# A fused attention, max-out and PReLU kernel: another order of the last batch's gate units and splits, and the first scores in two pairs of PSUM banks

## The chip, the cores and the metric

The kernel runs on one core of one Trainium2 chip. The metric is the device time of one execution in microseconds, from start to end, all loads and stores included. Smaller is better. In the texts below TensorE (PE in the rows) multiplies, VectorE (DVE), ScalarE (ACT) and GpSimd (POOL) work elementwise, and SP issues the DMAs.

## What is computed

Three layers follow one another. First comes attention over 4 batches, 8 heads, 576 positions and head width 64. Half of the heads look at the last 32 positions, the other half at every 32nd position:

```python
rel = pos[:, None] - pos[None, :]
mask_local = (rel >= 0) & (rel < stride)
mask_strided = (rel >= 0) & (pos[None, :] % stride == pos[:, None] % stride)
scores = np.where(masks, scale * q @ k.T, -1e9)
attn = softmax(scores) @ v
```

Its result, 2304 tokens by 512, goes through a max-out layer and then through a PReLU layer:

```python
h = np.maximum(np.maximum(x @ w1, x @ w2), x @ w3)    # 512 -> 768
y = h @ w_out                                         # 768 -> 512
g = np.maximum(y @ w_in, 0) + alpha * np.minimum(y @ w_in, 0)   # 512 -> 2048
out = g @ w_out2                                      # 2048 -> 512
```

All of it is float32. The kernel splits each factor of a large product into a high half (a cast, mostly on ScalarE) and a low half (a subtraction, mostly on VectorE), and takes three products, high by high, high by low and low by high.

## The kernel before

**The first stage, planned.** The attention of all batches, the first layer of batches 0 to 2 and the preparing of the weights are written as tasks. Each task has an engine, a cost, a due position, things it needs and gives, and ring slots (such as the 8 PSUM banks) it takes. The class `Weave` lists them in an order by simulating the engines with these costs (L108), and each engine then executes its tasks in that order. Costs count in nanoseconds: `COST = (250, 600, 500, 500)` are those of the local scores, local values, strided scores and strided values on TensorE; after a task of TensorE the plan waits 300, after one of ScalarE or VectorE 350, after a load 2300.

**A unit of strided attention** (`strided_tasks`, L439) is a batch and a pair of heads. Its scores are 24 matmuls (48 in the records, since a float32 matmul appears twice) into two PSUM banks, one for each head. They come in three groups i of two column blocks t each. For each group there is a mask task on VectorE (L475: add the mask, keep the row's maximum; four instructions) and an exponential task on ScalarE (L487: four instructions). Then follow normalisation, transposes, the product with the values, and the split of the result into x tiles, one for each half (`hf`) of the batch's positions and each 128 of the 512 model columns (`cc`). Before the first units' scores TensorE is given matmuls on a constant tile whose result nobody reads (L228). The first unit is u = (0, 2), batch 0 and `cc` 2; the second is (0, 3).

**Raw weights** arrive as 64-bit words and are taken apart on ScalarE and VectorE (L590 to L607) and then split (L283, L286). Three raw tiles are in flight.

**The last batch** (`last_net`, L844) follows the plan and is written out by hand, because its first layer is done in two ways. The gates of the first two of six f blocks are direct: a unit (hf, f, g) is one of 12 groups of 12 matmuls (L740), with `GATES_LAST` giving the order of (hf, f) and g running over the three gate matrices. Unit g = 0 is copied on ScalarE (L749), units 1 and 2 are maxima on VectorE that read the PSUM bank (L751), and after unit 2 the result h is split (L233, L236). The other four f blocks use Strassen's scheme with seven products of half size instead of eight (L922, 6 matmuls each), in the order 11, T2, 21, T3, T4, T1, 22. For them VectorE makes sums of x tiles, 16 operations called row sums (L863), four after each of the units 1 to 4. Then `make(m)` (L881) splits the eight sums: m = 0, 1 are T1 for the two halves of the model columns, 2, 3 are T2, 4, 5 are T3 and 6, 7 are T4. T4 is written into the x tiles of half 1 that the direct gate units read (`xt[b, i, 1]`). After unit n the calls are `make(n - 4)` for n from 4 to 9, and `make(6)`, `make(7)` follow the last unit. SP loads the Strassen weights after units 3, 5 and 7 (L896), and further ones later (`load_factors`).

**Beside it**, from the loop at L1126, which counts the same units n, the second layer's input of block 1 is made ready: loads into the tiles `xs` are issued at n = 2 and have to wait until the row sums and T1's split have read these tiles; at n = 8 GpSimd is given four subtractions (L1000), and from n = 10 on, every other n, a split whose low half is GpSimd's too (L236, `xst`).

**After the Strassen products** come 8 output products (L762, 18 matmuls each, a PSUM bank each), beside which ScalarE and VectorE split the second layer's first block (x2, L1150). The second layer (L1378 and on) fills the rest of the time.

**PSUM** is a ring of 8 banks (`bank()`, L274) up to the second layer; an allocation waits for the readers of the one eight before it.

## Time and profile before

| | us |
|---|---|
| median of 3 runs | 730.28 |
| lowest, highest | 729.89, 732.47 |
| the profiled execution, whole | 729.32 |
| its span, first to last instruction | 727.5 |
| TensorE busy | 716.7 |
| VectorE busy | 617.9 |
| ScalarE busy | 446.7 |
| mean granted TensorE clock, share of full | 0.997 |

The span is that of one execution. A busy TensorE is not TensorE at its pace: matmuls overlap, and their ends are modelled, so a stretch is read by how many matmuls it holds. In a row of a timeline, what stands in brackets at the end is how long the engine was idle before, and which instruction ended that. A line such as L236 can be that of a helper which several places call; the names of the tiles tell them apart.

### The profile page before, as it was taken

Reading aid. Unit: us, or ns where it says so; the run is one execution under the profiler, and the core shown is the slowest. Engines: PE = TensorE matmul, PEld = TensorE weight load, DVE = VectorE, ACT = ScalarE, POOL = GpSimd, SP = SyncE. Lnnn points to the kernel's source line nnn. Section 1 sums busy time; section 2 is a strip of 40 time slices with the busy share of each in tenths; the row PEclk is TensorE's granted clock in tenths of the full one; section 3 lists DMA queues with packets and bytes.
Section 4 is the critical chain, followed back from the end, with each engine's and each line's share of the span. In section 5 each row is a group of like instructions: output and inputs, shape, how many; then the busy total and the mean of one; then the engine's idle time right before and its main releaser. Section 6 shows DMA issues by size and latency. Waiting matters only on the chain.

```text
span 727.5 us, 18169 instructions
## 1 busy us (share of the span) xinstructions
PE 716.7 (99%) x6682; PEld 698.2 (96%) x6682; DVE 617.9 (85%) x1680; ACT 446.7 (61%) x1180; POOL 29.5 (4%) x53
## 2 busy tenths in 40 slices
PE   8999999999999999989999999999999999999998
PEld 5899999999999999989999999999999999999997
DVE  6988987987978997779878988979988888888896
ACT  7988976876776684233356575535566644656561
POOL 2000000000000000066000000000000000000000
PEclk9999999999999999999999999999999999999999
DMA  8787499878999778798998799999789999868362
GB/s 297 266 278 229 167 325 336 308 274 298 327 346 348 251 267 299 244 347 314 362 347 320 258 332 330 403 391 371 243 296 318 377 390 365 295 231 268 106 190 77
DMA packets 90089, 214.46 MB, mean 295 GB/s; under 512 B 11152, under 2 KB 41360, under 8 KB 90000
## 3 DMA queue, kind: packets, MB, share of 16 engines
q1 hardware_dynamic: 90000, 213.30, 83.2%
q8 instruction: 53, 0.87, 0.5%
q14 instruction: 36, 0.29, 0.1%
HBM read 157.16 MB, written 56.10 MB: 293 GB/s over the span
## 4 chain that ended last, share of the span: by engine, by line
PE 93%; DVE 2%; ACT 2%; DMA 2%; issue 0%; SPq 0%; ACTq 0%; DVEq 0%
PE ph L1378 24%; PE bank L740 23%; PE po L1179 15%; PE bank L762 11%; PE bank L922 4%; PE po L1185 4%; PE ph L1179 4%; PE po L1189 2%; PE bank L426 1%; PE bank L352 1%; PE bank L465 1%; ACT es L487 1%; PE bank L535 1%; DMA raw<-in_w 1%; DMA w<-ws 1%; DMA wo<-w 1%
## 5 line engine op out<-in xcount | busy, mean ns | idle before, releaser
L1378 PE MATMUL ph<-x,w 128*128 128x384 f32 x990 | 199.4, 336 | 0.0
L740 PE MATMUL bank<-x,w 128*128 128x288 f32 x1440 | 197.5, 296 | 0.6 <-ACT w L283 0.4
L740 PEld LDWEIGHTS bank<-x,w 128*128 128x128 f32 x1440 | 191.8, 188 | 2.2 <-ACT w L283 0.6
L1378 PEld LDWEIGHTS ph<-x,w 128*128 128x128 f32 x990 | 166.6, 188 | 0.8
L1179 PE MATMUL po<-w,g 128*128 128x256 f32 x936 | 135.8, 282 | 0.0
L1179 PEld LDWEIGHTS po<-w,g 128*128 128x128 f32 x936 | 130.1, 190 | 0.3
L1384 DVE TENSOR_TENSOR c<-ph,c 128x384 f32<-128x384 f32 x165 | 89.3, 553 | 31.1 <-PE ph L1378 30.4
L1172 ACT CAST g<-c 128x384 fp32r<-128x384 f32 x93 | 47.0, 505 | 91.3 <-DVE c L1362 52.3
L762 PE MATMUL bank<-h,w 128*128 128x288 f32 x576 | 80.1, 297 | 0.0
L762 PEld LDWEIGHTS bank<-h,w 128*128 128x128 f32 x576 | 77.0, 188 | 0.4
L286 DVE TENSOR_TENSOR w<-word,w 128x512 fp32r<-128x512 f32 x100 | 63.5, 643 | 14.0 <-ACT w L283 13.4
L283 ACT CAST w<-word 128x512 fp32r<-128x512 f32 x100 | 57.7, 588 | 25.7 <-DMA wp<-w 7.5
L1322 ACT ACTIVATE c<-c 128x384 f32<-128x384 f32 x96 | 50.5, 526 | 33.2 <-DVE c L1384 32.0
L1323 ACT ACTIVATE c<-c,nalpha 128x384 f32<-128x384 f32 x96 | 59.3, 617 | 3.1
L1327 DVE SCALAR_TENSOR_TENSOR c<-c 128x384 f32<-128x384 f32 x96 | 53.0, 552 | 5.9 <-ACT c L1323 5.9
L1173 DVE TENSOR_TENSOR g<-c,g 128x384 fp32r<-128x384 f32 x96 | 52.8, 550 | 0.9 <-ACT g L1172 0.5
L1173 DVE TENSOR_TENSOR g<-k,g 128x384 fp32r<-128x384 f32 x72 | 37.0, 551 | 7.4 <-ACT g L1172 7.4
L1185 PE MATMUL po<-w,g 128*128 128x512 f32 x120 | 42.8, 395 | 0.0
L830 DVE TENSOR_TENSOR t<-bank,t 128x288 f32<-128x288 f32 x72 | 32.6, 452 | 9.0 <-PE bank L740 5.6
L590 ACT ACTIVATE word<-raw 128x512 f32<-128x512 f32 x56 | 37.2, 678 | 4.1 <-DMA raw<-in_w 3.1
L922 PE MATMUL bank<-x,w 128*128 128x288 f32 x252 | 36.3, 305 | 2.6 <-DVE x L236 1.4
L922 PEld LDWEIGHTS bank<-x,w 128*128 128x128 f32 x252 | 35.3, 196 | 3.5 <-DVE x L236 2.1
(123 smaller groups left out, 905.3 us busy)
## 6 DMA issues: line engine op xcount, KB each, us to landing
w<-wh SPq DMA_DIRECT2D x72, 512.0 KB, 5.2
raw<-in_w SPq DMA_DIRECT2D x50, 512.0 KB, 5.2
w<-wo SPq DMA_DIRECT2D x48, 512.0 KB, 5.9
w<-wp SPq DMA_DIRECT2D x36, 512.0 KB, 6.3
wh<-w SPq DMA_DIRECT2D x24, 512.0 KB, 4.9
xd<-xst SPq DMA_DIRECT2D x28, 384.0 KB, 3.5
x<-xd SPq DMA_DIRECT2D x28, 384.0 KB, 8.4
ws<-w SPq DMA_DIRECT2D x12, 512.0 KB, 5.1
```

The source lines that it names most:

```text
L283: (nc.scalar.copy if e == "ACT" else nc.vector.tensor_copy)(out_, in_)
L286: nc.vector.tensor_tensor(out=out_, in0=x, in1=y, op=ALU.subtract)
L740: nc.tensor.matmul(acc, words["gate", f, g][:, wi, cc * P:(cc + 1) * P], xt[b, cc, hf][:, xi, :], start=n == 0, stop=n == 3 * NCC - 1)
L762: nc.tensor.matmul(acc, words["mix", f][:, wi, dc * P:(dc + 1) * P], st["h", hf, f][:, xi, :], start=n == 0, stop=n == 3 * NF1 - 1)
L922: nc.tensor.matmul(bank_, w[:, wi, off + c * P:off + (c + 1) * P], factors[name, c][:, xi, :], start=m == 0, stop=m == 5)
L1173: return g, lambda: nc.vector.tensor_tensor(out=g[:, 1], in0=x, in1=g[:, 0].bitcast(F32), op=ALU.subtract)
L1179: nc.tensor.matmul(bank[:, NH * half:NH * (half + 1)], g[:, gi, t * P:(t + 1) * P], w[:, wi, off:off + NH], start=first and i == 0, stop=l ...
L1185: nc.tensor.matmul(bank.rearrange("p (s n) -> p s n", n=NH), g[:, 0, t * P:(t + 1) * P], w[:, :, off:off + NH], start=first, stop=last)
L1323: nc.scalar.activation(a, a, AF.Copy, scale=nalpha[:, f:f + 1])
L1327: nc.vector.scalar_tensor_tensor(out=a, in0=h, scalar=0.0, in1=a, op0=ALU.max, op1=ALU.add)
L1378: nc.tensor.matmul(bank, words["h", n, i][:, wi, off + c * P:off + (c + 1) * P], x2h[blk, k, c][:, xi, :], start=m == 0, stop=m == 5)
L1384: nc.vector.tensor_tensor(out=out_, in0=bank, in1=other, op=ALU.add)
```

## The change

It has two parts.

The first is in the last batch. `GATES_LAST` goes from (0,0), (1,0), (0,1), (1,1) to (0,0), (1,0), (1,1), (0,1), so that both blocks of half 1 are done after unit 8 of 0 to 11. The splits of the token sums come after units 4 (one), 5 (two), 6 (two), 7 (one), 9 (one) and 10 (one) instead of one after each of the units 4 to 9 and two after the last.

The second is in the strided units. For the first one, (0, 2), the scores become two tasks, each with its own pair of PSUM banks: group 0 in the first, groups 1 and 2 in the second; a group's masks read the pair in which its scores are. For every strided unit the matmuls are now issued group by group instead of by g from 0 to 11.

```diff
--- before.py
+++ after.py
@@ -43,6 +43,7 @@
 WARM = 8
 UNREAD = {(0, 3): 2, (0, 0, 0): 2, (0, 1, 0): 3, ((0, 2), "t", 0): 4, ((0, 2), "s"): 2, ((0, 3), "s"): 3, (0, 0, 0, 0): 6}
 AFTER = {(1, 2): [("begun", 0, ("t", 0, 0, 0))]}
+PARTED = {(0, 2)}
 REDUCED = {(0, 2), (0, 3), (0, 0, 0), (0, 1, 0)}
 
 
@@ -446,34 +447,39 @@
         u = (b, cc)
         slack = 1500 if b else 0
         ek, qk, vk = ("es", u), ("q", b, cc), ("v", b, cc)
-        banks = [("sc", u, j) for j in range(2)]
-        cols = 6 * RW
-
-        def scores(_):
+        shares = ((0,), (1, 2)) if u in PARTED else ((0, 1, 2),)
+        banks = [[("sc", u, j, n) for j in range(2)] for n in range(len(shares))]
+
+        def scores(n):
             q, k = tl[qk]
-            sc = tl["sc", u] = [bank() for _ in range(2)]
-            unread(sc[0], UNREAD.get(u, 0))
-            tl[ek] = e_strided[turn[0] % 2]
-            turn[0] += 1
-            for name in ("mx", "ss", "sr"):
-                tl[name, u] = sm2.tile([P, 2, 6], F32, tag=name, name=name)
-            for g in range(12):
-                at = RW * min(g, NG2 - 1)
-                t = 2 * (g % 6 // 2) + g // 6
-                for j in range(2):
-                    rows = slice(D * j, D * (j + 1))
-                    nc.tensor.matmul(sc[j][D * (g % 2):D * (g % 2 + 1), RW * t:RW * (t + 1)],
-                                     q[rows, at:at + D], k[rows, at:at + RW], start=True, stop=True)
-
-        add((("PE", COST[2]),), scores, pos, needs=[qk], gives=[("sc", u)],
-            makes=[("bank", key) for key in banks] + [("es", ek)], uses=[qk], mode="scores")
+            sc = [bank() for _ in range(2)]
+            if n == 0:
+                unread(sc[0], UNREAD.get(u, 0))
+                tl[ek] = e_strided[turn[0] % 2]
+                turn[0] += 1
+                for name in ("mx", "ss", "sr"):
+                    tl[name, u] = sm2.tile([P, 2, 6], F32, tag=name, name=name)
+            for i in shares[n]:
+                tl["sc", u, i] = sc
+                for g in (2 * i, 2 * i + 1, 2 * i + 6, 2 * i + 7):
+                    at = RW * min(g, NG2 - 1)
+                    t = 2 * i + g // 6
+                    for j in range(2):
+                        rows = slice(D * j, D * (j + 1))
+                        nc.tensor.matmul(sc[j][D * (g % 2):D * (g % 2 + 1), RW * t:RW * (t + 1)],
+                                         q[rows, at:at + D], k[rows, at:at + RW], start=True, stop=True)
+
+        for n, part in enumerate(shares):
+            add((("PE", COST[2] * len(part) // 3),), lambda _, n=n: scores(n), pos,
+                needs=[qk] + ([("sc", u, 0)] if n else []), gives=[("sc", u, i) for i in part],
+                makes=[("bank", key) for key in banks[n]] + ([] if n else [("es", ek)]), uses=[qk], mode="scores")
         heads = (0, 1)
         for i in range(3):
             def masked(_, i=i):
                 for t in (2 * i, 2 * i + 1):
                     for j in heads:
                         nc.vector.tensor_tensor_reduce(
-                            out=tl[ek][:, j, t, :RW], in0=tl["sc", u][j][:, RW * t:RW * (t + 1)], in1=mask_s,
+                            out=tl[ek][:, j, t, :RW], in0=tl["sc", u, i][j][:, RW * t:RW * (t + 1)], in1=mask_s,
                             scale=-SCALE, scalar=3.0e38, op0=ALU.add, op1=ALU.min,
                             accum_out=tl["mx", u][:, j, t:t + 1])
                 if (u, i) == ((0, 2), 0):
@@ -486,7 +492,8 @@
                         sums = {} if u in REDUCED else dict(accum_out=tl["ss", u][:, j, t:t + 1])
                         nc.scalar.activation(e, e, AF.Exp, bias=tl["mx", u][:, j, t:t + 1], scale=-1.0, **sums)
 
-            add((("DVE", 4 * 133),), masked, pos, needs=[("sc", u)], gives=[("nm", u, i)], uses=banks + [ek])
+            add((("DVE", 4 * 133),), masked, pos, needs=[("sc", u, i)], gives=[("nm", u, i)],
+                uses=banks[i > 0 if u in PARTED else 0] + [ek])
             add((("ACT", 4 * (160 if u in REDUCED else 325)),), exponential, pos, needs=[("nm", u, i)],
                 gives=[("exp", u)], uses=[ek])
 
@@ -780,7 +787,7 @@
     GATES = [(0, 0), (0, 1), (0, 2), (1, 0), (0, 3), (0, 4), (1, 1), (0, 5), (1, 2),
              None, (1, 3), (1, 4), (1, 5), None]
     GATES_THEN = [what for what in GATES if what] + [None, None]
-    GATES_LAST = [(hf, f) for f in range(2 * NP // 3) for hf in range(2)]
+    GATES_LAST = [(0, 0), (1, 0), (1, 1), (0, 1)]
 
     def units(gates):
         hf = 0
@@ -890,14 +897,11 @@
                 for step in row_sums[:4]:
                     step()
                 del row_sums[:4]
-            if 4 <= n < 10:
-                make(n - 4)
+            for m in {4: (0,), 5: (1, 2), 6: (3, 4), 7: (5,), 9: (6,), 10: (7,)}.get(n, ()):
+                make(m)
             if n in (3, 5, 7):
                 load_factors(NP + n // 2)
             yield
-        for m in range(6, 8):
-            make(m)
-
         def add(out_, bank, other, op=ALU.add):
             nc.vector.tensor_tensor(out=out_, in0=bank, in1=other, op=op)
 
```

## Rows read from the trace of the kernel before

**Rows 1.** The page: busy time of each engine, share of the span, instructions.

```profile
PE 716.7 (99%) x6682; PEld 698.2 (96%) x6682; DVE 617.9 (85%) x1680; ACT 446.7 (61%) x1180; POOL 29.5 (4%) x53
```

**Rows 2.** Busy time by stretch: start:end length, engines (instructions), granted clock, DMA, GB/s.

```profile
0.00:35.00 35.00, 30.09 (x598) 23.87 (x602) 26.51 (x145) 28.68 (x99) 5.18 (x28) 1.00 0.81 279
35.00:291.60 256.60, 256.60 (x3157) 251.47 (x3149) 223.21 (x750) 190.35 (x607) 0.00 (x0) 1.00 0.84 290
...
310.65:317.50 6.85, 4.28 (x27) 3.35 (x25) 5.75 (x10) 3.39 (x10) 5.28 (x5) 0.99 0.96 364
317.50:321.00 3.50, 3.49 (x15) 3.49 (x16) 2.42 (x7) 1.05 (x3) 2.94 (x3) 0.52 0.99 396
```

**Rows 3.** Timeline, TensorE, the last batch's gate units: start, us, what, [idle before].

```profile
291.61 19.20 PE L740 MATMUL bank<-x,w 128*128 128x288 f32 x144
```

**Rows 4.** Timeline, TensorE, the first Strassen products.

```profile
310.65 2.68 PE L922 MATMUL bank<-x,w 128*128 128x288 f32 x19
313.83 0.67 PE L922 MATMUL bank<-x,w 128*128 128x288 f32 x3 [0.51 <-DVE x L236]
315.01 0.54 PE L922 MATMUL bank<-x,w 128*128 128x288 f32 x2 [0.51 <-DVE x L236]
316.73 0.40 PE L922 MATMUL bank<-x,w 128*128 128x288 f32 x1 [1.19 <-ACT x L233]
317.51 4.78 PE L922 MATMUL bank<-x,w 128*128 128x288 f32 x23 [0.37 <-DVE x L236]
```

**Rows 5.** Timeline, VectorE, the same stretch and just before.

```profile
307.72 0.45 DVE L751 TENSOR_TENSOR t<-bank,t 128x288 f32<-128x288 f32 x1
308.67 0.46 DVE L236 TENSOR_TENSOR h<-t,h 128x288 fp32r<-128x288 f32 x1 [0.50 <-ACT h L233]
...
312.52 2.44 DVE L236 TENSOR_TENSOR x<-t,x 128x288 fp32r<-128x288 f32 x2
314.88 1.01 DVE L751 TENSOR_TENSOR t<-bank,t 128x288 f32<-128x288 f32 x2
...
317.01 0.81 DVE L236 TENSOR_TENSOR x<-t,x 128x288 fp32r<-128x288 f32 x2
```

**Rows 6.** Timeline, GpSimd: first and third of its four subtractions.

```profile
311.26 1.02 POOL L1000 TENSOR_TENSOR t<-xs 128x384 f32<-128x384 f32 x1 [304.31 <-DVE t L751]
...
313.54 1.10 POOL L1000 TENSOR_TENSOR t<-xs 128x384 f32<-128x384 f32 x1
```

**Rows 7.** Timeline, ScalarE: T4's two high halves.

```profile
316.25 0.76 ACT L233 CAST x<-t 128x288 fp32r<-128x288 f32 x2
```

**Rows 8.** Timeline, VectorE and TensorE, the second layer's start.

```profile
364.30 0.55 DVE L236 TENSOR_TENSOR x<-xst,x 128x384 fp32r<-128x384 f32 x1
...
368.54 2.26 PE L1378 MATMUL ph<-x,w 128*128 128x384 f32 x12
```

**Rows 9.** Timeline, all engines, the first unit's scores and masks.

```profile
4.76 1.54 PE L465 MATMUL bank<-k,q 64*64 64x54 f32 x48
...
6.48 0.21 DVE L475 CUSTOM_DVE_ANT_0 es<-bank,mask_s 128x54 f32<-128x54 f32 x1 [5.48 <-PE bank L465]
...
7.14 0.92 PE L465 MATMUL bank<-k,q 64*64 64x54 f32 x48
...
8.11 0.21 DVE L475 CUSTOM_DVE_ANT_0 es<-bank,mask_s 128x54 f32<-128x54 f32 x1
...
17.12 0.95 DVE L286 TENSOR_TENSOR x<-bank,x 128x162 fp32r<-128x162 f32 x4 [0.55 <-ACT x L283]
```

**Rows 10.** Chain of work that ended last, first 35 us: start, us, what.

```profile
6.73 5.64 ACT es L487 x24
...
24.59 5.43 DMA raw<-in_w
...
32.02 1.62 PE bank L740 x10
```

## The prediction

> **What bounds the kernel now.** I read the page first: TensorE is busy for 99% of the span, VectorE for 85% [rows 1]. A kernel that is at its matmul pace nearly everywhere gains only where TensorE is not at that pace, so the second view is the busy time by stage [rows 2]. There the reader sees two places. In the first 35 us TensorE is busy 30.1 us, but with single small units and filler; until the first long run of gate products starts, the pace is set by the chain scores, masks, exponentials, weights. And in 310.65 to 317.50, where the last batch's Strassen products begin, it is busy 4.28 of 6.85 us, after which the granted clock is 0.52 for the next 3.5 us, that is near the lower level of 1.2 GHz against 2.4 GHz. From 35 to 291.6 us it is busy without a hole. The change touches exactly the two places, so I priced them and then asked whether a start won there reaches the end.
>
> **The matmul pace.** 144 gate products take 19.20 us, 0.1333 each [rows 3]. In 310.65 to 317.50 TensorE did 19 + 3 + 2 + 1 = 25 products [rows 4], worth 3.33 us: 3.5 us are lost to waiting. The slow clock costs (1 - 0.52) x 3.5 = 1.7 us more [rows 2]. Together 5.2 us is all that the second place can give back.
>
> **Why it waits there.** The waits are for the token sums' splits (VectorE L236): 0.51 and 0.51 us for the two of T3, then 1.19 for ScalarE's and 0.37 for VectorE's half of T4 [rows 4]. VectorE works in program order. Behind unit 5's maximum at 307.72 it splits T1, T2, takes two maxima, and gets to T3 only at 312.52; both T3 splits take 2.44 us instead of 2 x 0.46. Then come two maxima until 315.89, the low half of h, and at 317.01 T4 [rows 5]. The 2.44 us are GpSimd's doing: four subtractions run without a break from 311.26 on, some 1.15 us apart [rows 6], and VectorE's two-SBUF-input operations last until some 0.3 us after the running GpSimd one (312.52 + 2.44 = 314.96 against 313.54 + 1.10 = 314.64), while maxima that read PSUM keep their 0.45 to 0.5 pace.
>
> The Trainium skill (SBUF — State Buffer, section SBUF: two separate sides) calls this port pair an exclusive lock, held for the whole instruction, also against VectorE operations with two SBUF inputs. By that rule a caught split takes one GpSimd operation, 1.10 us; the row says 1.22, half of 2.44. The sum below goes by the row; by the rule, three caught splits would end 0.4 us sooner.
>
> **Part 1, the gate order and the splits.** Nothing is added or removed: 12 gate units, 16 row sums, 8 splits as before; no DMA is moved, and SP's loads at units 3, 5 and 7 keep their places. T1's first split stays at unit 4, which matters: the load of GpSimd's rows into the xs tiles waits for it, so GpSimd's start at 311.26 stays too (take that; were it bound to unit 8's maximum instead, it would start up to 0.8 us later, which helps). Up to 307.72 VectorE's order is unchanged. From there:
> - unit 5's maximum ends at 308.17; h's low half starts at 308.67 after the usual 0.50 wait for ScalarE [rows 5]. Then T1, T2, T2, T3 follow without maxima between. ScalarE gives a high half every 0.38 us at most (two in 0.76) [rows 7], VectorE takes 0.4 from start to start (two in 0.81) [rows 5]; T3's first low half starts at 310.4, unit 7's maximum at 310.75, T3's second at 311.1, done by 311.5, about when GpSimd starts.
> - TensorE needs T3 after three products, 18 x 0.1333 = 2.4 us behind 310.65: at 313.05. T3's two waits are gone, with 1.5 us of cover.
> - What is late next is T4, the fifth product, wanted at 313.85. Before it stand unit 8's maximum (to 311.95) and the low half of h (ready at 312.4), then T4's first split, unit 10's maximum and T4's second split. Three of these five have two SBUF inputs and fall into GpSimd's run. If the low half of h catches the end of GpSimd's first operation, the three end at about 312.9, 314.05 and 315.2; if it just misses it, one operation later, at 313.8, 314.95 and 316.1. With 0.3 us for the matmuls behind, T4 ends at 315.5 or 316.4 where the pace alone would give 314.65. The lost time is 0.9 to 1.8 us; I take the middle, 1.35: the rows don't say which it is, since low half and subtraction would start within 0.1 us of each other.
> - T4 may now be written early, since it overwrites x tiles of half 1 and those units end at unit 8. Behind T4's splits the maxima of units 10 and 11 come later than their own products by up to 6 us; who waits for them are the products that take their PSUM banks, eight allocations on: the last of this group at 316.8 and the first of the next at 317.6, against maxima done by 315.4 and 316.5. The cover is 1.1 us; without it the next group's first product would wait for unit 11's maximum.
> - The clock. Before, it fell after four idle stretches of 2.6 us in all within 313.3 to 317.5; now I expect two, of together 0.7 to 1.5 us. The first 35 us hold 4.9 us of idle time in pieces and keep 1.00 all through [rows 2]. So I take it that the clock holds, and keep its 1.7 us as a rival. The Trainium skill (TensorE: Matmul & The Clock Gate, section Why this matters for your kernels) warns only of a single long idle gap, by which the clock would hold here for sure; the trace disagrees, for its longest gap was 1.19 us and the clock fell all the same, so this rule is not used.
>
> Part 1 gives 5.2 - 1.35 = 3.9 us, between 3.4 and 4.3.
>
> **Does it reach the end?** Behind the Strassen products come the output products, then the second layer at 368.54. Its first product needs the x2 splits, the last of which that it reads runs at 364.30 to 364.85 [rows 8]. This leaves 3.7 us if those splits don't move at all; their loads are issued from TensorE's own progress, so they move with it for the most part. I take 0.2 off, with 0 to 0.7 as bounds: 3.7 us for part 1. After that TensorE has no hole of its own, and nothing takes the start back.
>
> **Part 2, the first unit's scores.** The 48 recorded matmuls take 1.54 us from 4.76, and the first mask starts at 6.48, after all of them [rows 9]. With a bank pair for the first third, the first four masks need 16 of 48, some 0.5 to 0.7 us: they start at 5.45 to 5.65 and the exponentials, 24 in a row from 6.73 [rows 10], about 0.85 us earlier. Masks 5 to 12 of the unit wait for the second pair at 6.48 as before, and ScalarE has four exponentials (0.94 us) to bridge. What is hidden: the second unit's masks start at 8.11 because its scores run at 7.14 to 8.06 [rows 9], and those wait for their loads; so VectorE gains nothing there. From 8.11 on VectorE's order has one hole, 0.55 us at 17.12, and that is a wait for ScalarE [rows 9]. ScalarE being 0.6 to 0.85 us early, this hole closes: 0.55 us. The chain from there goes over VectorE's word joins to the raw weights' load issued at 24.59, its landing 5.43 us later and the first dense products at 32.02 [rows 10], each of which starts when the one before ends. I take 0.5 us; 0 if the load lands when it did (the queue has other loads in it), 0.85 at most.
>
> The two added bank allocations move the ring by two. By the planner's own costs the two shares (166 + 333 for 500) bring the first masks and exponentials forward by 334 of its nanoseconds, but VectorE's tasks behind the second unit's scores keep their planned starts, and ScalarE's lead is used up at the next masks it must wait for: the order on each engine stays, worked out by hand. The ring's shift also moves the second layer's first two banks onto output units that are copied out earlier (the second and third of eight rather than the fourth and fifth), which helps if anything. The other units' changed order of groups costs nothing: a mask waits for the whole unit in any case.
>
> **Sum.** 3.7 + 0.5 = 4.2 us. The profiled execution's own time is 729.32 us (span 727.5 and 1.8 around it): 725.1. It stands 0.96 us below the median of the runs shown, 730.28, which is what a run is compared with: 726.1 us.
>
> **Rivals.**
> - *The clock falls again* in T4's shorter stall: 1.7 us less, 4.2 - 1.8 = 2.4 gained, 727.9. For it: two idle stretches remain, close together. Against: less than 60% of the idle time before. 0.15.
> - *The lock keeps the stall*: T3's second split is caught too, everything shifts by one more GpSimd operation, T4's second split ends at 317.1, as late as before, and the clock falls. Lost 2.75 + 1.7 instead of 5.2; with part 2, 1.3 us gained, 729.0. This is the skill's lock rule at its worst alignment; the row of 2.44 us shows it can hold two splits running. 0.12.
> - *Part 2 does nothing*, the load landing when it did: 726.6. 0.07.
> - *Slower*: my hand-worked plan is wrong, and the two shares put a load of values or of the next batch ahead of a raw weight load. One such load is 5.43 us from issue to landing [rows 10], and up to 6.1 with the queue full; it decides once the loss passes the 4.2 us gained: 730.3 - 3.7 + 6.1 = 732.7. Against it: nothing in the plan's first 9 us competes with those loads. 0.06.
>
> The forecast itself keeps 0.60, with 725.0 to 727.4 as its own range (3.4 + 0 - 0.7 up to 4.3 + 0.85).
>
> **How the numbers follow.** 0.5% is 3.65 us, about what a measurement of this kernel can tell from no change; it puts the line at 726.6, within the forecast's own range. Three quarters of the forecast lie below it, and half of the third rival: 0.60 x 0.75 + 0.07 x 0.5 = 0.48, rounded to 0.5. Slower by over 0.5% needs a loss of 7.3 us behind the gain: 0.03. The rest is within. The range for 8 in 10 goes from the forecast's best (4.3 + 0.85 and some scatter of the runs, 724.8) to the second rival (729.0).
>
> **What would show it.** In the profile after: the first mask at about 5.5 and the 24 exponentials from about 5.8; VectorE's 0.55 us hole gone and the first dense products near 31.5; no wait of TensorE for T3; its waits for T4 together below 1.6 us; granted clock 1.00 throughout 310 to 325; the second layer's first product about 4 us earlier. The prediction is wrong if GpSimd's subtractions start earlier and catch T3, if the clock still falls, if TensorE waits at the second layer's start for x2 splits or loads, or if the order of the attention tasks differs beyond the first unit.

## The result and the profile after

| | before | after |
|---|---|---|
| median of 20 executions, us | 730.02 | 734.27 |
| lowest and highest, us | 728.22, 732.47 | 730.47, 737.06 |
| the profiled execution, us | 729.32 | 732.71 |
| its span, us | 727.5 | 730.9 |

The kernel after is slower: the ratio of the times is 1.0054, with a 95% interval of 1.0043 to 1.0065, that is 3.9 us (3.1 to 4.7). The prediction was 726.1 in a range of 724.8 to 729.0, with 0.03 for slower by over 0.5%.

TensorE's timeline of the kernel after from the first Strassen products on (start, us, line, what, number of matmuls, [idle before, and what ended it]) stands beside [rows 4] and [rows 8]. L926 are the Strassen products, L769 the output products, L1382 the second layer's first:

```profile
309.68 4.00 PE L926 MATMUL bank<-x,w 128*128 128x288 f32 x28
314.20 30.20 PE L926 MATMUL bank<-x,w 128*128 128x288 f32 x224 [0.52 <-DVE x L237]
344.24 2.59 PE L769 MATMUL bank<-h,w 128*128 128x288 f32 x15
347.62 0.40 PE L769 MATMUL bank<-h,w 128*128 128x288 f32 x1 [0.79 <-ACT h L939]
348.25 17.20 PE L769 MATMUL bank<-h,w 128*128 128x288 f32 x128 [0.23 <-DVE h L913]
370.06 3.89 PE L1382 MATMUL ph<-x,w 128*128 128x384 f32 x12 [4.61 <-ACT xo L982]
373.78 2.27 PE L1382 MATMUL po<-x,w 128*128 128x384 f32 x12
```

The same stretch of the kernel before, which [rows 4] and [rows 8] show in part, went on like this; there is no wait anywhere in it:

```profile
317.51 32.02 PE L922 MATMUL bank<-x,w 128*128 128x288 f32 x227 [0.37 <-DVE x L236]
349.37 19.33 PE L762 MATMUL bank<-h,w 128*128 128x288 f32 x144
...
370.64 2.24 PE L1378 MATMUL po<-x,w 128*128 128x384 f32 x12
```

Here the reader can follow the whole difference between these two executions. The Strassen products start 0.97 us earlier (309.68 against 310.65) and take 34.56 us instead of 38.72: 5.1 us won, as foreseen. The output products take 21.21 us instead of 19.33, and 1.9 are gone; the rows show 1.02 of it as waits for h. The lead is 3.25 us at their end (365.45 against 368.70). Then TensorE stands for 4.61 us before the second layer's first product, and its first two products, 12 matmuls, take 3.72 us to the next row instead of 2.10. From there (373.78 against 370.64) the kernel is 3.14 us behind, and 3.4 at the end (730.9 against 727.5).

What it waits for is "ACT xo": ScalarE's copy of an output unit. ScalarE's rows of the kernel after:

```profile
320.31 0.51 ACT L234 CAST xst<-xs 128x384 fp32r<-128x384 f32 x1 [3.79 <-DMA xd<-xst]
320.73 0.39 ACT L944 COPY t<-bank 128x288 f32<-128x288 f32 x1
...
347.13 0.43 ACT L939 CAST h<-t 128x288 fp32r<-128x288 f32 x1 [1.38 <-DVE t L906]
...
354.42 0.51 ACT L234 CAST x<-xs 128x384 fp32r<-128x384 f32 x1 [4.23 <-DMA xs<-x]
...
364.71 0.39 ACT L982 COPY xo<-bank 128x288 f32<-128x288 f32 x1
...
366.24 0.99 ACT L982 COPY xo<-bank 128x288 f32<-128x288 f32 x3
369.61 0.40 ACT L982 COPY xo<-bank 128x288 f32<-128x288 f32 x1 [2.37 <-DMA x<-xo]
```

and of the kernel before:

```profile
350.36 0.43 ACT L935 CAST h<-t 128x288 fp32r<-128x288 f32 x1 [1.39 <-DVE t L902]
...
354.73 0.51 ACT L233 CAST x<-xs 128x384 fp32r<-128x384 f32 x1 [1.30 <-DMA xs<-x]
...
365.07 0.39 ACT L978 COPY xo<-bank 128x288 f32<-128x288 f32 x1
...
366.60 1.00 ACT L978 COPY xo<-bank 128x288 f32<-128x288 f32 x3
369.22 0.40 ACT L978 COPY xo<-bank 128x288 f32<-128x288 f32 x1 [1.62 <-DMA x<-xo]
369.80 0.48 ACT L1388 COPY c<-ph 128x384 f32<-128x384 f32 x1 [0.18 <-PE ph L1378]
```

The last of the eight output copies waits for a tile: they have a ring of four, so it takes the tile of the fourth copy, and that one's store (DMA x<-xo) has to land first. That holds the last copy until 369.22 before and 369.61 after. It hardly depends on when TensorE comes: on ScalarE the fourth copy (365.07 and 364.71) stands behind splits of the x2 rows, and these begin when the rows land, at 354.73 before and at 354.42 after. TensorE began the output products 5.1 us earlier, the rows came 0.3 earlier.

Before, no matmul needed the bank that the last copy empties until the third product, at 370.64. After, the second layer's first product does. Which bank a tile gets is fixed when the program is built. By the built programs' addresses the eight output units have banks 7, 3, 2, 5, 1, 6, 4, 0 before and 1, 0, 7, 3, 4, 5, 2, 6 after, and the second layer's first product has bank 6 in both. So before it follows the sixth output unit, copied within the group at 366.60, and after it follows the last. The banks don't simply go round a ring of eight, as the text ahead of the prediction has it: the two programs part at the 21st bank that they take, and from there the banks follow in another order, not only two places on. Part 1 alone (e1) has the banks of before, part 2 alone (e2) those of after.

The windows of the kernel after (start:end length, busy time of TensorE, its weight loads, VectorE, ScalarE and GpSimd, granted clock, DMA share, GB/s), of which the first two answer to [rows 2]:

```profile
310.65:317.50 6.85, 6.33 (x46) 6.00 (x46) 5.57 (x10) 3.78 (x10) 6.62 (x7) 1.00 1.02 396
317.50:321.00 3.50, 3.50 (x28) 3.50 (x27) 1.84 (x5) 0.69 (x2) 1.74 (x3) 1.00 1.03 404
344.00:364.00 20.00, 18.88 (x138) 18.20 (x138) 13.55 (x31) 6.67 (x17) 0.54 (x1) 1.00 0.96 341
364.00:378.00 14.00, 9.39 (x48) 9.16 (x48) 6.21 (x15) 5.35 (x14) 0.46 (x1) 0.88 0.98 334
```

The fall of the clock at 317.5 is gone, and another has come behind the 4.61 us of idleness: 0.88 in the mean over 14 us, which is the 1.6 us by which the 12 matmuls are late. The DMA column is close to 1 in all four rows.

### The profile page after: what moved, and what is told of

The parts are those of the page before. It is cut to its first block, busy times and chain, and to the rows that moved or that the text cites. A ratio compares the mean times of both kernels' runs of the same rounds, so it can differ in the third digit from the quotient of the medians.

```text
span 730.9 us, 18172 instructions
## 1 busy us (share of the span) xinstructions
PE 716.2 (98%) x6682; PEld 697.8 (95%) x6682; DVE 615.8 (84%) x1680; ACT 446.5 (61%) x1180; POOL 30.6 (4%) x53
## 4 chain that ended last, share of the span: by engine, by line
PE 90%; DMA 5%; DVE 1%; ACT 1%; POOL 0%; SPq 0%; issue 0%; ACTq 0%; DVEq 0%; POOLq 0%
PE ph L1382 24%; PE bank L747 23%; PE po L1183 15%; PE bank L769 10%; PE po L1189 4%; PE ph L1183 4%; PE bank L926 2%; PE po L1193 2%; DMA w<-ws 1%; PE bank L427 1%; PE bank L353 1%; DMA w<-wh 1%; PE bank L229 1%; PE bank L469 1%; PE bank L542 1%; DMA k<-in_kTl 1%
## 5 line engine op out<-in xcount | busy, mean ns | idle before, releaser
L1382 PE MATMUL ph<-x,w 128*128 128x384 f32 x990 | 201.1, 338 | 4.6 <-ACT xo L982 4.6
L747 PE MATMUL bank<-x,w 128*128 128x288 f32 x1440 | 197.6, 296 | 0.2 <-DVE w L287 0.2
L747 PEld LDWEIGHTS bank<-x,w 128*128 128x128 f32 x1440 | 191.9, 188 | 1.7 <-DVE w L287 0.4
L1382 PEld LDWEIGHTS ph<-x,w 128*128 128x128 f32 x990 | 168.0, 190 | 6.0 <-ACT xo L982 4.8
L769 PE MATMUL bank<-h,w 128*128 128x288 f32 x576 | 80.8, 297 | 1.1 <-ACT h L939 0.8
L769 PEld LDWEIGHTS bank<-h,w 128*128 128x128 f32 x576 | 77.1, 188 | 2.2 <-ACT h L939 1.0
L1366 DVE TENSOR_TENSOR k<-c 128x384 f32<-128x384 f32 x72 | 37.8, 549 | 0.0
L1176 ACT CAST g<-k 128x384 fp32r<-128x384 f32 x72 | 33.1, 514 | 7.1 <-PE ph L1183 3.2
```

The costliest lines, as they stand in the source:

```text
L747: nc.tensor.matmul(acc, words["gate", f, g][:, wi, cc * P:(cc + 1) * P], xt[b, cc, hf][:, xi, :], start=n == 0, stop=n == 3 * NCC - 1)
L769: nc.tensor.matmul(acc, words["mix", f][:, wi, dc * P:(dc + 1) * P], st["h", hf, f][:, xi, :], start=n == 0, stop=n == 3 * NF1 - 1)
L1176: cast(g[:, 0], x)
L1382: nc.tensor.matmul(bank, words["h", n, i][:, wi, off + c * P:off + (c + 1) * P], x2h[blk, k, c][:, xi, :], start=m == 0, stop=m == 5)
```

## The experiments

Theory: the bank of the second layer's first product is the loss, and part 2's two added allocations put it there. Rivals: the x2 rows and their splits would hold the second layer at 370 whatever the bank; ScalarE's last copy is the limit, bank or not; one part of the change costs by something else. All ratios are against the kernel before on the same chip. Where two variants are compared, the text divides their ratios; the intervals of both then count.

| kernel | median, us | ratio to before, 95% interval |
|---|---|---|
| part 1 alone, e1 | 732.03 | 1.0012 (0.9992 to 1.0031) |
| part 1 alone again, e12 | 729.79 | 0.9991 (0.9978 to 1.0003) |
| part 2 alone, e2 | 732.80 | 1.0025 (1.0009 to 1.0041) |
| part 2 alone, free banks, e11 | 729.30 | 0.9998 (0.9980 to 1.0015) |
| before, first product in the last bank, e4 | 733.88 | 1.0044 (1.0027 to 1.0061) |
| after, a tile for the last copy, e6 | 731.47 | 1.0014 (0.9999 to 1.0029) |
| after, free banks, e3 | 730.02 | 0.9995 (0.9979 to 1.0010) |
| after, free banks and the tile, e5 | 729.27 | 0.9978 (0.9962 to 0.9993) |
| free banks, three splits later, e8 | 728.86 | 0.9968 (0.9953 to 0.9984) |
| free banks, no GpSimd work, e9 | 728.06 | 0.9959 (0.9942 to 0.9976) |
| free banks, 4 of 28 early stores, e7 | 726.00 | 0.9945 (0.9920 to 0.9969) |
| free banks, the tile, splits later, e10 | 727.07 | 0.9953 (0.9937 to 0.9970) |

**Part 1 alone (e1).** The kernel after with the first unit's scores in one pair of banks:

```diff
-PARTED = {(0, 2)}
+PARTED = set()
```

> Part 1 alone: the new gate order and the earlier splits, the first unit's scores in one pair of banks as before. In this kernel the PSUM banks of the late units fall as in the kernel before: the second layer's first product takes the bank of the sixth output unit, its third product that of the last. Bank theory (the loss comes from the second layer's first product sitting in the bank of the LAST output unit, which part 2's two extra allocations bring about): TensorE comes to the second layer 4.3 us early, at about 366.4, starts product 0 without the 4.61 us wait at 366.5 to 367, but stands before product 2 until the last output copy, at about 370 as before. Gain 0 to 1.5 us against the kernel before, about 729.4. Rival (the order change itself costs, for example by later x2 splits): slower than the kernel before by 1 us or more, with product 0 near 370.

Measured 0.9 us slower, with an interval that holds no difference. Its profile fell on an execution in which the clock fell far ahead of the change's place, at the end of the first stage. That window, and TensorE's first Strassen products:

```profile
30.00:35.00 5.00, 4.01 (x43) 3.31 (x44) 3.21 (x6) 4.53 (x10) 0.00 (x0) 0.69 1.03 381
```

```profile
311.85 3.33 PE L926 MATMUL bank<-x,w 128*128 128x288 f32 x24
```

The Strassen products began 2.2 us later than in the kernel after, GpSimd began at 315.06, and T4 was caught again. So this run decides nothing, and the program was run once more (e12, below).

**Part 2 alone (e2).** The kernel after with the gate order and the splits of before:

```diff
-GATES_LAST = [(0, 0), (1, 0), (1, 1), (0, 1)]
+GATES_LAST = [(0, 0), (1, 0), (0, 1), (1, 1)]
-for m in {4: (0,), 5: (1, 2), 6: (3, 4), 7: (5,), 9: (6,), 10: (7,)}.get(n, ()):
+for m in {4: (0,), 5: (1,), 6: (2,), 7: (3,), 8: (4,), 9: (5,)}.get(n, ()):
...
+for m in range(6, 8):
+    make(m)
```

> Part 2 alone: the first unit's scores in two pairs of banks, gate order and splits as before. The second layer's first product takes the bank of the last output unit. Bank theory: the dense products start 1.0 us earlier, the Strassen stall with the 0.52 clock is there as before, and product 0 waits for the last output copy, to about 369.6, where the kernel before started at 368.54: 1.1 us slower if the clock holds in the 2 us of waiting, 2.7 us if it falls. Rival (part 2 harmless, the loss comes from the order change): 0.5 to 1.0 us faster than before.

1.8 us slower, within what the bank theory gave; the rival, 0.5 to 1.0 faster, falls. TensorE at the second layer's start:

```profile
348.88 19.23 PE L769 MATMUL bank<-h,w 128*128 128x288 f32 x144
369.83 2.37 PE L1385 MATMUL ph<-x,w 128*128 128x384 f32 x12 [1.72 <-ACT xo L985]
```

The same wait for the same copy, without part 1's lead. It is shorter by the lead that is missing, and there is no slow clock behind it.

**The kernel before with the bank of after (e4).** One index, by which products 0, 1 and 2 of the first pass change places; product 0 gets the last output unit's bank:

```diff
-bank = banks[(1, 0, 3, 2)[k % 4] % len(banks)]
+bank = banks[((3, 0, 1, 2) if n == 0 else (1, 0, 1, 0))[k % 4]]
```

> The kernel before, with one index changed: the second layer's first product goes into the bank of the last output unit instead of the sixth. Nothing else is touched. Bank theory: TensorE ends the output products at 368.5 as before and then waits for the last output copy (369.22 to 369.6 in the trace of before): product 0 at 369.7 instead of 368.54, and the copy of product 0 and all behind it move by the same 1.1 us: 0.8 to 1.6 us slower than before. Rival (the bank was incidental, another wait would stand there): no difference.

3.2 us slower (2.0 to 4.5): the sign is right, the size twice what was expected. TensorE, then ScalarE:

```profile
371.24 1.34 PE L1378 MATMUL po<-x,w 128*128 128x384 f32 x6 [2.71 <-ACT xo L978]
```

```profile
370.79 0.40 ACT L978 COPY xo<-bank 128x288 f32<-128x288 f32 x1 [3.33 <-DMA x<-xo]
```

In this execution the store landed later and the last copy started at 370.79 instead of 369.22; that moment isn't fixed. With the bank put right behind it, each delay of that store becomes a delay of the kernel: product 0 starts 2.70 us later than in the trace of before (368.54). This is the loss of the change reproduced in a kernel that has nothing else of it.

**The kernel after with free banks (e3).** The second layer's first pass has four banks of the output pool, and takes them first:

```diff
-banks += [ps_o.tile([P, DM], F32, tag="po", name="po")[:, :HB] for _ in range(2)]
+banks += [ps_o.tile([P, DM], F32, tag="po", name="po")[:, :HB] for _ in range(4)]
-bank = banks[(1, 0, 3, 2)[k % 4] % len(banks)]
+bank = banks[(2, 3, 4, 5, 0, 1, 2)[k]] if n == 0 else banks[(1, 0, 3, 2)[k % 4] % 2]
```

> The kernel after, but the second layer's first pass takes four banks of the output pool and two of the hidden pool in an order in which products 0 to 3 land in the banks of the second, sixth, fifth and fourth output units, and the last output unit's bank comes fifth. Bank theory: the 4.61 us wait before product 0 is gone, it starts when the output products end (365.5) or the x2 splits are done (364.5 to 365.5), and the clock stays up; ScalarE's copy of product 0 still comes behind the last output copy (370.0), so VectorE's chain starts at 370.5 rather than 373. Gain 4 to 6 us against the kernel after, 1.5 to 3 against before: about 727.5. First rival (the x2 rows and splits hold the second layer at about 370 whatever the bank): same as the kernel after, with the wait now for VectorE's splits. Second rival (ScalarE's last output copy, which waits 2.37 us for a tile whose store is under way, is what sets everything, bank or not): TensorE starts early but stands later behind VectorE, gain under 1.5 us against the kernel after.

Against the kernel after it is faster by the ratio of the two ratios, 0.9995 / 1.0054: 4.3 us (about 2.9 to 5.7), as the bank theory gave. The first rival falls, since product 0 starts without a wait, and so does the second, which allowed 1.5 us. Against the kernel before it gains 0.4 us where 1.5 to 3 were expected: the interval holds 0. TensorE shows where the rest of the lead went:

```profile
334.85 10.67 PE L926 MATMUL bank<-x,w 128*128 128x288 f32 x78 [0.93 <-ACT t L944]
345.35 1.76 PE L769 MATMUL bank<-h,w 128*128 128x288 f32 x12
347.63 1.02 PE L769 MATMUL bank<-h,w 128*128 128x288 f32 x3 [0.52 <-ACT h L939]
349.45 0.40 PE L769 MATMUL bank<-h,w 128*128 128x288 f32 x1 [0.80 <-ACT h L939]
350.08 17.22 PE L769 MATMUL bank<-h,w 128*128 128x288 f32 x128 [0.23 <-DVE h L913]
367.14 4.35 PE L1382 MATMUL po<-x,w 128*128 128x384 f32 x24
```

4.0 us ahead of before when the output products start, it is 1.4 ahead (368.54 against 367.14) when they end: it waits for a ScalarE copy and for the last h. The last output copy (368.92) and behind it the copy of product 0 (369.21) still wait for the store, so that copy is only 0.59 earlier than before (369.80). Up to the output products' end this is the same work as in the kernel after, whose trace has no wait at 334.85 and ends them at 365.45: 1.9 us lie between two executions here. Three suspects for the lost lead were tried on this kernel.

**Without most of the early stores (e7).**

```diff
 for blk, k, i, t in early_parts:
-    nc.sync.dma_start(xd[blk][k][i], t.bitcast(F32))
+    if k == 0:
+        nc.sync.dma_start(xd[blk][k][i], t.bitcast(F32))
...
-    nc.sync.dma_start(t.bitcast(F32), xd[blk][k][i])
+    nc.sync.dma_start(t.bitcast(F32), xd[blk][0][i])
```

> The free-bank variant of the kernel after, with 24 of the 28 early stores of the second block's splits left out (only those of the first product are stored, and all products are fetched from these; the output is not the reference's). It asks why TensorE's lead of 4 us at the start of the output products is 1.4 us at their end. Store theory: ScalarE's early splits wait for these stores (2.3 to 4.6 us in three places of the traces, on a full DMA), ScalarE's copies of the Strassen products queue behind them, VectorE waits for the copies and gives the last h late. Without the stores ScalarE's waits go, TensorE's waits for h at the start of the output products (1.55 us in the free-bank variant) fall below 0.6 us, and the x2 rows land earlier too, since there is less traffic: 1.5 to 4 us faster than the free-bank variant. Lock theory (GpSimd's work holds VectorE up): waits for h stay, at most 0.5 us faster. Third (the x2 rows' round trip through DRAM sets the second layer's start whatever comes before): the waits for h go, but a wait of the same size shows at the second layer's first product.

The text on record speaks of the second block's stores. The program has 28 early stores, 14 for the second block and 14, through the same helper, for the third; the edit leaves out 12 of each.

3.65 us faster than the free-bank variant (about 1.5 to 5.8), and the wait for h is 0.24. TensorE, then ScalarE:

```profile
345.03 2.69 PE L769 MATMUL bank<-h,w 128*128 128x288 f32 x16
347.96 17.22 PE L769 MATMUL bank<-h,w 128*128 128x288 f32 x128 [0.24 <-DVE h L913]
365.02 4.34 PE L1383 MATMUL po<-x,w 128*128 128x384 f32 x24
```

```profile
346.84 0.43 ACT L939 CAST h<-t 128x288 fp32r<-128x288 f32 x1 [1.38 <-DVE t L906]
...
365.26 0.40 ACT L982 COPY xo<-bank 128x288 f32<-128x288 f32 x1 [1.98 <-PE bank L769]
```

Both numbers are those of the store theory, and the lock theory's, at most 0.5, falls here. The row at 320.31 of the kernel after shows a way from a store to h: ScalarE stands 3.79 us before an early split whose tile is still being stored, and its copy of a Strassen product (L944, 320.73) stands behind in program order; VectorE and then h follow from that copy.

But the trace doesn't show that the stores cost the kernel after its 1.9 us. The h that TensorE waits for has its high half at 346.84 here and at 347.13 in the kernel after: 0.29 earlier without most of the stores. The wait is short because TensorE came 0.79 later (345.03 against 344.24). With ScalarE's waits gone, VectorE's own work holds this h nearly as long. What is plain in the trace is the other end: the x2 loads are issued at 340.03 instead of 347.23, the fourth output copy runs at 358.67 instead of 364.71, and the last one waits for TensorE and no longer for a store.

**Three early splits behind the copy (e8).**

```diff
-ready = {X_SPLIT + 22 * half + 2 * k: (1, half, k) for half in range(2) for k in range(7)}
+ready = {X_SPLIT + 22 * half + 2 * k + (half == 0 and k > 3): (1, half, k) for half in range(2) for k in range(7)}
...
```

> The free-bank variant of the kernel after, with the last three early splits of the first half one unit later, so that on ScalarE the copy of the second Strassen group's first product comes ahead of the split that waits 3.8 to 4.6 us for a store. Store theory: VectorE's wait of 1.5 to 2.3 us at 319 to 322 is gone and its chain is that much earlier at first; the second half's splits still stand ahead of the sixth group's copy (343.3), so TensorE's waits at the output products shrink by no more than half: 0 to 1 us faster than the free-bank variant. Lock theory: VectorE's operations slow down in the same places, no difference.

2.0 us faster than the free-bank variant, where 0 to 1 was expected, at the edge of what two intervals of 1.1 us each can tell, and 2.3 (1.2 to 3.4) faster than the kernel before. The two profiled executions take the same time (spans of 726.6 and 726.4), so they don't show where the gain lies. VectorE's wait at 319 to 322 is gone; the wait of 0.79 us for h, to which the second half's splits belong, is there as expected. What is late next is the next pass's first product: it waits for VectorE to empty its bank, VectorE for ScalarE's copy of product 0 (369.52), and that stands behind the last output copy at 369.23:

```profile
374.05 1.31 PE L1382 MATMUL ph<-x,w 128*128 128x384 f32 x6 [0.97 <-DVE c L1388]
```

**Without GpSimd's work (e9).** The row sums on GpSimd are left out, the splits read the rows, and the high half is stored twice, as two transfers of half the size in place of each store:

```diff
-        split(t[:, 0], t[:, 1], xs.pop((blk, PRODUCTS[k][1], i)), nc.scalar, lo_engine)
+        if lo_engine is nc.gpsimd:
+            nc.scalar.copy(t[:, 0], x)
...
+            for r in range(2):
+                nc.sync.dma_start(xd[blk][k][i][:, r, :], t[:, 0, :].bitcast(F32))
```

> The free-bank variant of the kernel after, without GpSimd's work in the last batch: the second block's row sums and low halves are left out (the splits read the rows themselves, and the high half is stored twice, so that the bytes stored are the same; the output is not the reference's). Lock theory: VectorE's operations with two SBUF inputs keep 0.45 us between 309 and 345 (they take 0.65 on average in the trace of the free-bank variant, 3 to 5 us in all), the T4 splits are in time, TensorE's waits in the Strassen products and for h go: 1.5 to 4 us faster than the free-bank variant. Store theory: the T4 stall of 0.52 goes, but ScalarE's waits for stores and VectorE's for ScalarE stay, at most 1 us faster.

2.6 us faster than the free-bank variant (intervals of 1.1 and 1.2 us), more than the store theory gave it. But the profile doesn't speak for the lock alone. TensorE no longer waits for T4, and still waits for h; ScalarE's waits for stores are longer than in the kernel after. TensorE, then ScalarE:

```profile
309.42 24.59 PE L926 MATMUL bank<-x,w 128*128 128x288 f32 x174
...
347.89 0.40 PE L769 MATMUL bank<-h,w 128*128 128x288 f32 x1 [0.79 <-ACT h L939]
348.53 17.20 PE L769 MATMUL bank<-h,w 128*128 128x288 f32 x128 [0.24 <-DVE h L913]
```

```profile
321.69 0.51 ACT L1020 CAST xst<-xs 128x384 fp32r<-128x384 f32 x1 [5.38 <-DMA xd<-xst]
```

TensorE ends the output products at 365.7, where the kernel after ended them at 365.45 with GpSimd at work. The 0.52 us at T4 went with GpSimd's work. How the rest of the 2.6 us divides isn't settled, also because the stores are now twice as many.

**The kernel after with a tile for the last copy (e6).** The bank is left where it is; the tile comes from a pool of its own:

```diff
-xo = tp.tile([P, HALF], F32, tag="t", name="xo")
+xo = (xo_p if NCC * hf + dc >= 7 else tp).tile([P, HALF], F32, tag="t", name="xo")
...
```

> The kernel after with one thing more: the last output unit has a tile of its own for its copy, so that ScalarE doesn't wait for a store (2.37 us in the trace of after) before it empties the bank. The second layer's first product is still in that unit's bank. Bank theory as it stands now (product 0 waits for the LAST copy, and that copy waits for a store on a full DMA): the last copy runs right behind the three before it, at 367.3 instead of 369.6, product 0 starts at 367.7 after 2.2 us of waiting instead of 4.6, with less or no slow clock: 2.4 to 4 us faster than the kernel after, 730 to 732. Rival (the store isn't what the copy waits for, or product 0 waits for something else): under 1 us faster.

2.9 us faster than the kernel after (1.0014 / 1.0054, about 1.5 to 4.3). The last copy runs in a pair with the seventh, and product 0 waits 1.07 us instead of 4.61, with the clock up. TensorE, then ScalarE:

```profile
367.23 2.35 PE L1384 MATMUL ph<-x,w 128*128 128x384 f32 x12 [1.07 <-ACT xo L982]
```

```profile
366.48 0.70 ACT L982 COPY xo<-bank 128x288 f32<-128x288 f32 x2 [0.50 <-DMA x<-xo]
```

Another bank takes the wait away, an earlier copy shortens it to 1.07: the loss needed both, the bank and the late copy.

**Free banks and the tile (e5).** Both edits together.

> As the free-bank variant of the kernel after, and the last output unit has a tile of its own for its copy, so that ScalarE needn't wait for a store to land. Bank theory: the last output copy runs right behind the other three at about 367.3, ScalarE's copy of product 0 at 367.7, and nothing is late any more; against the free-bank variant alone 0 to 1 us faster (726.5 to 727.5). Second rival (the last copy is the limit): 2.4 us or more faster than the free-bank variant, which then gained little.

1.6 us faster than before (0.5 to 2.8), and 1.2 less in time than the free-bank variant, with intervals that hold 0 difference; the time, 729.27, is 2 us over what was expected. The second rival, 2.4 us or more over the free-bank variant, isn't borne out. Its profile fell on an execution with a fall of the clock at 10 to 15 us, so its second layer's start isn't read here.

**All three repairs (e10).** Free banks, the tile, the three splits later.

> All three repairs on the kernel after: free banks for the second layer's first products, a tile of its own for the last output copy, and three early splits of the first half behind the copy on ScalarE. Theory: each takes away a wait that was seen for itself (4.61 us before product 0, 0.5 to 1.0 us before product 5, 1.5 to 2.3 us of VectorE), nothing new comes late; TensorE keeps the 3.25 us by which it ends the output products earlier: 727.0 to 728.0, that is 2.5 to 3.5 us faster than the kernel before and 0 to 1.5 faster than the variant without the tile. Rival (DMA sets the start of the second layer, through the x2 rows that land at 353 to 355 in nearly all traces): no faster than the variant without the tile (728.9).

3.4 us faster than the kernel before (2.2 to 4.6) and 7.4 (0.0101 of 730) faster than the kernel after: it beats both. It takes 1.1 us less than e8, whose interval overlaps with its own. TensorE has no wait at the second layer's start:

```profile
348.49 17.22 PE L769 MATMUL bank<-h,w 128*128 128x288 f32 x128 [0.24 <-DVE h L913]
365.55 4.34 PE L1384 MATMUL po<-x,w 128*128 128x384 f32 x24
```

The first x2 rows were there at 354.4, as in the kernel after, and did not hold it back: in the trace that rival falls, as far as TensorE's start goes. The time doesn't exclude it, since 1.1 us against e8 is within the two intervals. The three edits were not tried on the kernel before, so no run shows how much of the 3.4 us the change itself brings.

**Part 2 alone with the free banks (e11).**

> Part 2 alone (the first unit's scores in two pairs of banks), with the free banks for the second layer's first products. Bank theory: the 1.8 us that part 2 alone lost are the bank; without it its 1.0 us earlier start of the dense products is left: 0.5 to 1.2 us faster than the kernel before, 2 to 3 us faster than part 2 alone. Rival (the two pairs cost something elsewhere): slower than the kernel before still.

2.0 us faster than part 2 alone (0.9998 / 1.0025, about 0.2 to 3.7), and no difference to the kernel before, where 0.5 to 1.2 us less were expected; the interval, 1.5 less to 1.1 more, holds the expected gain too. In its profile product 0 starts at 367.28 against 368.54 before, and against 369.83 in e2:

```profile
367.28 4.34 PE L1385 MATMUL po<-x,w 128*128 128x384 f32 x24
```

That the bank was what part 2 lost is borne out; what part 2 wins by itself is too small for this measurement.

**Part 1 alone once more (e12).**

> Part 1 alone once more, word for word the same program: its first profile fell on an execution in which the clock fell at 30 to 35 us and GpSimd began 5 us later than in the trace of after, so that it doesn't show what part 1 does by itself. Theory (part 1 wins 4 us in the Strassen products; the waits for h and the last copies take back most): TensorE begins the output products 3 to 4.2 us early relative to the start of the Strassen products, and the second layer 0.5 to 2 us early relative to it; 0 to 1.5 us faster than the kernel before, 729 to 730.5. Rival (without part 2 the order change is worth nothing): the Strassen products take 37 us or more from first to last, as in the first profile, and no difference or slower.

0.7 us faster (1.6 less to 0.2 more), within the theory's 0 to 1.5, with an interval that holds no difference. TensorE, then the window from 344 to 364 us:

```profile
310.47 4.00 PE L926 MATMUL bank<-x,w 128*128 128x288 f32 x28
...
345.11 2.73 PE L769 MATMUL bank<-h,w 128*128 128x288 f32 x15
348.62 0.40 PE L769 MATMUL bank<-h,w 128*128 128x288 f32 x1 [0.79 <-ACT h L939]
349.25 18.73 PE L769 MATMUL bank<-h,w 128*128 128x288 f32 x128 [0.23 <-DVE h L913]
367.82 2.27 PE L1382 MATMUL ph<-x,w 128*128 128x384 f32 x12
```

```profile
344.00:364.00 20.00, 18.89 (x126) 18.07 (x125) 14.16 (x31) 7.21 (x18) 1.28 (x2) 0.91 1.01 350
```

The output products begin at 345.11, 34.64 us behind the Strassen products' start instead of 38.72: 4.1 won, so the rival, 37 or more, falls. The second layer begins 57.35 us behind it instead of 57.89: 0.5 left. Between them lie the waits for h and, in this execution, a fall of the clock: 128 matmuls take 18.73 us, where 17.20 were enough in the kernel after.

## Why the prediction was wrong

**The first stage went as foretold, its size isn't shown.** The first mask starts at 5.39 and the exponentials at 5.65 (said: 5.45 to 5.65, and 5.8). The first dense products start at 31.01 instead of 32.02: 1.0 us won where 0.5 was taken, with 0.85 at most. Part of that is chance: e4 runs the program of before up to here, and its first mask starts at 5.86 and its dense products at 31.45. Seven other kernels with the two pairs (e2, e3, e6 to e9, e11) have them between 30.63 and 30.99, and e10 has them at 31.79. The time of e11 shows no gain. The other units' order stayed.

**The Strassen stall was right, and a little pessimistic.** Both waits for T3 are gone, T4's are 0.52 us where 0.9 to 1.8 were expected, and the clock holds at 317.5. The output products begin 5.1 us earlier, of which 0.97 are the earlier start. GpSimd did start earlier, at 310.09, and caught T4's splits (1.02 and 0.89 us instead of 0.46) and not T3's. In the rivals' arithmetic one sum is off: slower by over 0.5% takes 4.2 + 3.65 = 7.9 us, not 7.3, which moves no bound.

**The step that failed is the way from the won start to the second layer**, in three places: one sentence of part 2 on the banks, and two of "Does it reach the end?".

- "The ring's shift also moves the second layer's first two banks onto output units that are copied out earlier". The banks don't go round a ring. Before, the first two products had the banks of the sixth and the first output unit (not the fourth and fifth), after those of the last and the third: the first product's bank moved to the latest copy of all, not to an earlier one. This is the term that turned the sign: e4 puts it into the kernel before by itself and costs 3.2 us, e3 takes it out of the kernel after and gives back 4.3. None of the rivals was this one; the slower rival laid the loss on a load in the first stage.
- "This leaves 3.7 us if those splits don't move at all". The slack was read from VectorE's splits alone [rows 8]. The other thing that the second layer's start needs is ScalarE's queue, with the output copies in it. The rows of before that are shown above would have told it: the last copy runs at 369.22, behind a store, and behind it ScalarE waits only 0.18 us for product 0. On ScalarE the slack was 0.18 us. By those rows the sum's 3.7 would have been a fraction of one, unless the copies moved, and they depend on a store that landed 3.8 us after the fourth copy. Nor did the splits "move with it for the most part", which the sum priced at 0.2: the one at 364.30 moved to 363.94, 0.36 for TensorE's 5.1. That alone would have done no harm, since TensorE was ready at 365.45.
- "After that TensorE has no hole of its own, and nothing takes the start back". The output products gave 1.9 us back before the second layer, waiting for the last h. Before, h was ready in time; its high half came at 350.36. After, it came at 347.13, 3.2 us earlier, where TensorE came 5.1 earlier. Which work holds this h isn't shown: without most of the stores (e7) its high half came at 346.84, with three splits moved (e8) at 347.11, without GpSimd's work (e9) at 347.41. In e3, from which these three were made, it came at 348.96, so two executions of the same work differ by more than any of the three moves it against the kernel after, which is 0.3 us at most.

**The clock** was priced in the right place and fell in another: behind the 4.61 us of idleness, at 1.6 us. In the same window, 364 to 378, waits of 1.07 (e6), 1.72 (e2) and 2.71 us (e4) before the first product left it at 1.00. The Trainium skill (TensorE: Matmul & The Clock Gate, section Why this matters for your kernels) warns of a single long idle gap. The fall behind 4.61 us agrees with that; the fall that e12 shows, with gaps of 0.79 and 0.23 us in the rows before it, that rule wouldn't have foretold, and there the measurement decides. The Trainium skill, same title, section A second HAM failure mode: psum-queue depth-cycling, tells of a clock that swings when matmul groups idle briefly and often, for bf16. That is nearer to what the row shows; no run here settles whether it is the same.

**A gain was there to be had.** e10 wins 3.4 us with the same change and three small edits behind it, near the 4.2 predicted. The prediction had none of these three. Whether the edits would win something without the change was not tried.

## What to carry to other kernels

A start won in one stage is worth what the tightest queue behind it has left, and every engine's queue has to be read for that: here VectorE had 3.7 us and ScalarE 0.18. What doesn't move with the start, here rows that landed 0.3 us earlier for a lead of 5.1, fixes that slack. When a change adds a buffer allocation anywhere, look up in the built program which tile now shares its memory with which; a first use behind a last release is a wait that no line of the source shows. And a copy that frees a bank shouldn't wait for a store: one more tile of output room was worth 2.9 us in the kernel after.

## What the runs showed that was not expected

**One program, other clock falls.** The kernel after and e12 run the same work through the output products with the same waits (0.79 and 0.23 us), and the granted clock was 1.00 in the one and 0.91 over 20 us in the other. In e1 it fell at 30 to 35 us (0.69), in e5 at 10 to 15 us (0.79), and in the twelve other traces, of before and after among them, it didn't fall in the first 35 us. An estimate from these rows, the missing share of the clock times the length of the window, is 1.1 to 1.8 us for each such fall, which is as much as the effects measured here: a single profile of a program can show a place where others of its executions don't lose anything.

**The landing of a store wanders.** The last output copy, which waits for one, started between 368.9 and 370.8 in traces of kernels with the ring of four and much the same stage before it (before 369.22, after 369.61, e3 368.92, e4 370.79). From the end of the fourth copy that is 3.8, 4.5, 4.9 and 5.5 us. Nothing shows it as long as nobody waits for it.
